# A fused attention and two-MoE kernel: which VectorE operation a GpSimd operation at the shared port waits for

## The chip, the cores and the metric

One core of a Trainium2 chip. The metric is the device time of one execution in microseconds; the time of a kernel is the median of its runs. Every row of a profile comes from one profiled execution. Engines are named as in the profile: PE (TensorE matmul), PEld (its weight load), DVE (VectorE), ACT (ScalarE), POOL (GpSimd), SP (SyncE, which issues the DMAs).

## The reference

Three parts follow one another. The attention has 4 batches of 8 heads, 576 positions, 64 channels; scores below the row's maximum less `tau` are cut off before the softmax:

```python
scores = scale * np.matmul(q, k.transpose(0, 1, 3, 2))
thresh = np.max(scores, axis=-1, keepdims=True) - tau
scores = np.where(scores >= thresh, scores, -1000000000.0)
attn = softmax(scores)          # exp of the difference to the maximum, divided by the sum
x = matmul(attn, v)             # then laid out as 2304 tokens x 512
x = g(x @ w_in) @ w_out         # g(h) = h * clip(h + 3, 0, 6) / 6;    512 -> 2048 -> 512
out = g2(x @ w2_in) @ w2_out    # g2(h) = h / (1 + exp(-1.702 h));     512 -> 2048 -> 512
```

## The kernel before

The data are float32. To use the faster float32r matmul, an operand is split into a high part (rounded, by ScalarE or VectorE) and a low part (the difference, a subtraction by GpSimd or VectorE), and a product is three matmuls: high by high, high by low, low by high. The weights arrive as 64-bit numbers and are decoded on the chip (`decode`, L559): two copies on ScalarE, three operations on VectorE (L586, L587, L588) and an addition on GpSimd (L589); then they are split (`split`, `split_to`, `combined`).

In time there are three stages. Up to about 410 us the heads are worked in 16 pairs (`unit`, L721): scores on TensorE, maximum and masked exponentials on VectorE and ScalarE (`soft`, L838), the sums' reciprocals and the scaling on GpSimd and VectorE (`norm`, L861), a transposition, the product with V, and the first half of the first MoE (`moe_a`, L1099) mixed in between. From 410 to 650 us the second half of the first MoE runs (`moe_b`, `wide`), while the second MoE's weights are decoded and combined. From 650 us on the second MoE runs in blocks of 512 tokens (one of 256), each with seven products of half-size matrices in place of eight (`moe2`, `hidden2`, `gate2`; their sums and differences `c`, `u`, `p` are made by VectorE and GpSimd).

No engine's order is left to a scheduler. Each operation is entered in a `Plan` (L178) with its engine, a cost, what it reads and writes, and sometimes an alternative engine; `SWAPS` picks the alternatives. `Plan.order` (L229) goes through time with these costs and the latencies `LAT` between engines (L25; from VectorE to GpSimd 155), picks the next operation of each engine by a stored rank (`RANKS`), and leaves a planned start for each. The program is written out in the order of these starts. The sets `PORT` (L35) name the operations that use the SBUF port which VectorE and GpSimd share: while one engine has such an operation, the planner does not start one on the other (L262), and lets it start at exactly the moment the other one ends:

```python
if port[o] and taken[DVE + POOL - e] > t:
    est[o] = taken[DVE + POOL - e]
```

`Plan.fill` (L369) is what carries this into the program. For each GpSimd operation at the port (L394) it looks up the last VectorE operation (of any kind) whose entry in `ends` is not after the GpSimd operation's planned start (plus 0.5), and `tie` (L1628) adds a semaphore wait for it. VectorE is not made to wait for GpSimd in this way. `ends` is what the change touches; `busy` (L1634), also called from `fill`, puts a few idle matmuls into the first 60 us.

Of the kernel before, what the change touches and what calls it, by code (L numbers as in the profile page):

```python
# [22 lines left out]
PE, ACT, DVE, POOL, SP, DMA = range(6)  # L23

LAT = {  # L25
    (PE, PE): 0, (PE, ACT): 197, (PE, DVE): 197, (ACT, PE): 200, (ACT, ACT): 200, (ACT, DVE): 150, (ACT, POOL): 170,
    (DVE, PE): 200, (DVE, ACT): 120, (DVE, DVE): 127, (DVE, POOL): 155, (POOL, PE): 203, (POOL, ACT): 200, (POOL, DVE): 220, (POOL, POOL): 130,
    (SP, DMA): 53, (ACT, DMA): 53, (DMA, PE): 943, (DMA, ACT): 943, (DMA, DVE): 943, (DMA, POOL): 1000, (DMA, SP): 943,
}
# [148 lines left out]
class Plan:  # L178
# [190 lines left out]
    def fill(self, order, make):  # L369

        made, dve = {}, [o for o in order if o.eng == DVE]
        ends = [self.start[o.n] + o.cost + LAT[DVE, POOL] for o in dve]

        def keep(op):
            return lambda: made.__setitem__(op.n, op.fn())

        def behind(op, i):
            return lambda: self.tie(op.fn(), next((made[o.n] for o in dve[i::-1] if made[o.n] is not None), None))

        used = [[] for _ in range(BANKS)]  # L380
        for b in self.banks:
            ops = [x[0] for x in b.access]
            used[b.bank].append((min(self.start[o.n] for o in ops), max(self.start[o.n] + o.cost for o in ops) + 250))
        out, end = [], 0.0
        for op in order:
            if op.eng == PE:
                t, s = end, self.start[op.n]
                end = max(end, s + op.cost)
                count = int((s - t) / 450 if s < 12000 else (s - t - 300) / 216)
                if count > 0:  # L390
                    slack = max((min([t - y for _, y in u if y <= t] + [1e9]), -i) for i, u in enumerate(used) if not any(x < s and y > t for x, y in u)) if any(not any(x < s and y > t for x, y in u) for u in used) else None
                    if slack is not None:
                        out.append(make(-slack[1], count))
            i = bisect_right(ends, self.start[op.n] + 0.5) - 1 if op.eng == POOL and self.port[op.n] else -1  # L394
            out.append(keep(op) if op.eng == DVE else behind(op, i) if i >= 0 else op.fn)
        return out
# [1301 lines left out]
```

## Time and profile before

| what | value |
| --- | --- |
| median of 3 runs (1028.32, 1028.89, 1031.9) | 1028.89 us |
| profiled execution, its own time | 1031.23 us |
| its span, first to last instruction | 1029.4 us |
| TensorE busy | 1016.6 us |
| VectorE busy | 792.3 us |
| ScalarE busy | 667.9 us |
| GpSimd busy | 566.3 us |

Busy time is time in which an engine has an instruction under way; a record of GpSimd or VectorE also holds the time in which it stands at the port. Matmuls are pipelined and each record is longer than the distance to the next, so a TensorE that is busy in the records can still lose a little between matmuls. In the list of waits a row names who waited, for whom, the sum in us, how often, and the longest. A wait for several semaphores is put down to the one that came last. In the timeline a row is: start, duration, engine, line, operation, out<-in, and in brackets the idle time of the engine before it with what ended it. Operations that a helper makes carry the helper's line (L534 is `tt`, L531 is `copy`), so they are told apart by their tiles.

### The profile page before, as it was taken

Reading aid. Unit: us, or ns where it says so; the run is one execution under the profiler, and the core shown is the slowest. Engines: PE = TensorE matmul, PEld = TensorE weight load, DVE = VectorE, ACT = ScalarE, POOL = GpSimd, SP = SyncE. Lnnn points to the kernel's source line nnn. Section 1 sums busy time; section 2 is a strip of 40 time slices with the busy share of each in tenths; the row PEclk is TensorE's granted clock in tenths of the full one; section 3 lists DMA queues with packets and bytes.
Section 4 is the critical chain, followed back from the end, with each engine's and each line's share of the span. In section 5 each row is a group of like instructions: output and inputs, shape, how many; then the busy total and the mean of one; then the engine's idle time right before and its main releaser. Section 6 shows DMA issues by size and latency. Waiting matters only on the chain.

```text
span 1029.4 us, 21355 instructions
## 1 busy us (share of the span) xinstructions
PE 1016.6 (99%) x7560; PEld 950.0 (92%) x7560; DVE 792.3 (77%) x1700; ACT 667.9 (65%) x1395; POOL 566.3 (55%) x681
## 2 busy tenths in 40 slices
PE   8999999999999999999999999999999999999998
PEld 7787888798979898999999999999999999999998
DVE  7999999997999994667876687656677997555544
ACT  5988678676777674766444344667757767555553
POOL 5577866675756562666564435445654535446452
PEclk9999999999999999999999999999999999999999
DMA  8344466686877665445746778937464896443412
GB/s 242 118 118 126 140 186 189 170 233 171 223 212 200 199 188 165 143 142 182 206 149 178 242 230 266 310 105 258 148 204 168 280 317 198 143 165 110 144 45 73
DMA packets 113195, 187.47 MB, mean 182 GB/s; under 512 B 10816, under 2 KB 62656, under 8 KB 111040
## 3 DMA queue, kind: packets, MB, share of 16 engines
q1 hardware_dynamic: 112944, 185.80, 58.7%
q8 instruction: 60, 0.98, 0.4%
q14 instruction: 47, 0.39, 0.1%
q10 hardware_dynamic: 144, 0.29, 0.1%
HBM read 117.77 MB, written 68.29 MB: 181 GB/s over the span
## 4 chain that ended last, share of the span: by engine, by line
PE 90%; DVE 4%; DMA 2%; ACT 1%; POOL 1%; issue 1%; SPq 0%; DVEq 0%; POOLq 0%; ACTq 0%
PE pm L1306 18%; PE py L1442 11%; PE pm L1072 11%; PE py L1097 10%; PE pm L1097 8%; PE pm L1187 7%; PE pm L1442 6%; PE ps L792 6%; PE pm L1010 5%; PE pm L918 3%; PE ps L816 1%; PE pm L994 1%; DVE e L852 1%; PE ps L832 1%; DVE nm L848 1%; DMA wrawstg<-in_w1o_dram 1%
## 5 line engine op out<-in xcount | busy, mean ns | idle before, releaser
L848 DVE TENSOR_REDUCE nm<-ps 128x1 f32<-128x576 f32 x144 | 106.2, 750 | 14.9 <-PE ps L792 10.2
L851 ACT ACTIVATE e<-ps,nm 128x576 f32<-128x576 f32 x128 | 93.2, 740 | 30.1 <-DVE nm L848 26.9
L534 POOL TENSOR_TENSOR g<-t,g 128x256 fp32r<-128x256 f32 (+2 forms) x84 | 74.4, 888 | 65.4 <-ACT g L531 19.1
L852 DVE SCALAR_TENSOR_TENSOR e<-ps,th,e 128x576 f32<-128x576 f32 x128 | 102.1, 811 | 6.9 <-ACT e L851 3.6
L1097 PE MATMUL pm<-g,outhring 128*128 128x256 f32 (+1 forms) x512 | 105.7, 299 | 0.0
L531 ACT ACTIVATE g<-t 128x256 fp32r<-128x256 f32 (+3 forms) x177 | 86.1, 489 | 20.9 <-DVE t L1084 10.5
L1072 PE MATMUL pm<-xh,inhring 128*128 128x256 f32 (+1 forms) x320 | 97.8, 306 | 0.3 <-DVE t L1084 0.2
L1097 PE MATMUL py<-g,outhring 128*128 128x432 f32 (+2 forms) x384 | 96.8, 336 | 0.0
L1072 PE MATMUL pm<-xh,inlring 128*128 128x256 f32 (+1 forms) x320 | 94.4, 295 | 0.0
L1072 PE MATMUL pm<-xl,inhring 128*128 128x256 f32 (+1 forms) x320 | 94.4, 295 | 0.0
L534 POOL TENSOR_TENSOR wmstg<-wmstg,wrstg 128x512 uint32<-128x512 uint32 x40 | 54.2, 1358 | 72.4 <-DVE wmstg L588 32.3
L792 PE MATMUL ps<-kqv 128*128 128x288 f32 x480 | 82.0, 302 | 2.2 <-DVE th L849 1.1
L1097 PEld LDWEIGHTS pm<-g,outhring 128*128 128x128 f32 x512 | 81.9, 189 | 0.8 <-issue 0.5
L792 PEld LDWEIGHTS ps<-kqv 128*128 128x128 f32 x480 | 68.2, 190 | 10.0 <-issue 4.5
L1097 PE MATMUL pm<-g,outlring 128*128 128x256 f32 (+1 forms) x256 | 75.6, 295 | 0.0
L1097 PEld LDWEIGHTS py<-g,outhring 128*128 128x128 f32 x384 | 68.7, 188 | 2.1
L1097 PE MATMUL py<-g,outlring 128*128 128x432 f32 (+2 forms) x192 | 64.6, 336 | 0.0
L1072 PEld LDWEIGHTS pm<-xh,inhring 128*128 128x128 f32 x320 | 60.6, 189 | 2.1 <-PE pm L1639 0.5
L1072 PEld LDWEIGHTS pm<-xl,inhring 128*128 128x128 f32 x320 | 60.6, 189 | 0.0
L534 POOL TENSOR_TENSOR kqv<-qk,kqv 64x576 fp32r<-64x576 f32 (+1 forms) x39 | 55.9, 1434 | 8.4 <-DVE g L534 2.5
L1072 PEld LDWEIGHTS pm<-xh,inlring 128*128 128x128 f32 x320 | 60.5, 189 | 0.0
L1358 ACT ACTIVATE pm<-id 128x256 f32<-128x256 f32 (+1 forms) x98 | 37.4, 387 | 30.8 <-DVE c L534 30.3
(265 smaller groups left out, 3615.9 us busy)
## 6 DMA issues: line engine op xcount, KB each, us to landing
turned<-tr SPq DMA_DIRECT2D x16, 1024.0 KB, 4.1
et<-turned SPq DMA_DIRECT2D x64, 256.0 KB, 5.7
wrawstg<-in_w1i_dram SPq DMA_DIRECT2D x16, 512.0 KB, 4.0
wrawstg<-in_w1o_dram SPq DMA_DIRECT2D x16, 512.0 KB, 3.6
wrawstg<-in_w2i_dram SPq DMA_DIRECT2D x16, 512.0 KB, 4.0
wrawstg<-in_w2o_dram SPq DMA_DIRECT2D x16, 512.0 KB, 4.2
qk<-in_k_dram SPq DMA_DIRECT2D x24, 288.0 KB, 3.9
qk<-in_q_dram SPq DMA_DIRECT2D x24, 288.0 KB, 4.3
```

The costliest lines, as they stand in the source:

```text
L531: return lambda: nc.scalar.activation(out=o(), in_=i(), func=ACTF.Copy, **kw)
L534: return lambda: (nc.vector if eng == DVE else nc.gpsimd).tensor_tensor(out=o(), in0=a(), in1=b(), op=op)
L792: nc.tensor.matmul(ps.t[:, i, :SH], q, w[hd].t[:, i * SH:(i + 1) * SH], start=a, stop=z)
L848: add(DVE, 672, K("R", s), "R", lambda: nc.vector.tensor_reduce(out=nm.t[:, c], in_=ps.t[:, :, :SH], op=ALU.max, axis=AX.XY, negate=True), ...
L851: add(ACT, 624, K("X", s), "X", lambda: nc.scalar.activation(out=ev(), in_=ps.t[:, :, :SH], func=ACTF.Exp, bias=nm.t[:, c]), [ps, (nm, s)] ...
L852: add(DVE, 736, K("M", s), "M", lambda: nc.vector.scalar_tensor_tensor(out=ev(), in0=ps.t[:, :, :SH], scalar=th.t[:, c], in1=ev(), op0=ALU ...
L1010: nc.tensor.matmul(pv[p].t[64 * hd:64 * hd + 64, :CH[p][1]], v_(k, hd), et_m(p, turned)[:, hd, k], start=k == 0, stop=False)
L1072: nc.tensor.matmul(ph.t[:, :n], a, v, start=(cc == 0 and i == 0), stop=(cc == KC - 1 and i == 2))
L1097: nc.tensor.matmul(py.t[:, :n], a, v, start=(st and i == 0), stop=(sp and i == 2))
L1187: nc.tensor.matmul(ph.t[:, :n], a, v, start=(cc == 0 and q == 0), stop=(cc == KC - 1 and q == 2))
L1306: nc.tensor.matmul(half(i)(), u.t[:, ws], v.t[:, xv], start=False, stop=True, skip_group_check=True)
L1442: nc.tensor.matmul(to, u.t[:, ws], v.t[:, at:at + n], start=(st and j == 0 and cc == 0 and o is not None), stop=(sp and j == 2), skip_grou ...
```

## The change

The latency from VectorE to GpSimd is no longer added to the planned end of a VectorE operation in `fill`. The lookup for a GpSimd operation can then find a later VectorE operation: one that is planned to end up to 155 before the GpSimd operation's planned start, or exactly at it. Ranks, costs, planned starts and the order of every engine stay as they are.

```diff
     def fill(self, order, make):
 
         made, dve = {}, [o for o in order if o.eng == DVE]
-        ends = [self.start[o.n] + o.cost + LAT[DVE, POOL] for o in dve]
+        ends = [self.start[o.n] + o.cost for o in dve]
 
         def keep(op):
             return lambda: made.__setitem__(op.n, op.fn())
```

## Rows read from the trace of the kernel before

**Rows 1.** The page's first part: busy us, share of the span, instructions.

```profile
PE 1016.6 (99%) x7560; PEld 950.0 (92%) x7560; DVE 792.3 (77%) x1700; ACT 667.9 (65%) x1395; POOL 566.3 (55%) x681
```

**Rows 2.** Busy us by stage: stretch, length, engines, PEclk, DMA share, GB/s.

```profile
0.00:60.00 60.00, 56.30 (x361) 44.12 (x362) 52.59 (x135) 45.06 (x83) 32.55 (x58) 1.00 0.57 171
60.00:250.00 190.00, 187.71 (x1432) 160.88 (x1431) 175.93 (x429) 147.40 (x301) 134.01 (x192) 1.00 0.61 173
250.00:410.00 160.00, 158.77 (x1215) 140.31 (x1214) 136.58 (x324) 105.84 (x219) 87.12 (x145) 1.00 0.68 190
410.00:650.00 240.00, 239.80 (x1453) 233.50 (x1452) 179.37 (x341) 128.73 (x239) 130.44 (x108) 1.00 0.63 194
650.00:1029.00 379.00, 374.06 (x3110) 371.22 (x3108) 247.88 (x473) 240.86 (x557) 182.17 (x179) 1.00 0.53 177
```

Engines in each row: PE, PEld, DVE, ACT, POOL.

**Rows 3.** The page's chain that ended last, by engine.

```profile
PE 90%; DVE 4%; DMA 2%; ACT 1%; POOL 1%; issue 1%; SPq 0%; DVEq 0%; POOLq 0%; ACTq 0%
```

**Rows 4.** Waits of TensorE from 0 to 410 us, two of ten.

```profile
PE ps L792 <- DVE th L849: 1.1, 1, 1.1
...
PE ps L816 <- DVE th L849: 0.8, 1, 0.8
```

**Rows 5.** Waits of TensorE from 410 us to the end, all of them.

```profile
PE pm L1306 <- ACT pm L1358: 0.7, 2, 0.3
PE pm L1072 <- DVE t L1084: 0.2, 1, 0.2
```

**Rows 6.** Timeline at 837 us: VectorE, GpSimd and ScalarE.

```profile
836.87 0.68 DVE L534 TENSOR_TENSOR outlring<-outlring,outhring 128x512 fp32r<-128x512 f32 x1
...
837.48 0.68 DVE L534 TENSOR_TENSOR gl<-c,g 128x512 fp32r<-128x512 f32 x1
...
837.70 1.06 POOL L534 TENSOR_TENSOR c<-t,c 128x256 f32<-128x256 f32 x1 [5.15 <-DVE outlring L534]
...
838.79 0.63 ACT L531 ACTIVATE g<-c 128x512 fp32r<-128x512 f32 x1 [0.37 <-POOL c L534]
```

**Rows 7.** GpSimd's operations on tile c: count, ns min/median/max, first and last.

```profile
L534 POOL TENSOR_TENSOR c<-t,c x28: 727/790/1192, 665.0 to 997.3; 128x256 f32<-128x256 f32 x28
```

**Rows 8.** Timeline at 433 us: VectorE, then GpSimd.

```profile
433.37 0.69 DVE L588 SCALAR_TENSOR_TENSOR wmstg<-wrawstg,wmstg 128x512 uint32<-128x512 uint32 x1
...
434.13 1.41 POOL L534 TENSOR_TENSOR wmstg<-wmstg,wrstg 128x512 uint32<-128x512 uint32 x1 [1.45 <-DVE wmstg L588]
```

**Rows 9.** Timeline at 514 us: VectorE, GpSimd and TensorE.

```profile
514.62 0.41 DVE L587 TENSOR_SCALAR wmstg<-wmstg 128x512 uint32<-128x512 uint32 x1
514.85 1.17 POOL L534 TENSOR_TENSOR g<-t,g 128x432 fp32r<-128x432 f32 x1 [0.83 <-DVE yc L534]
515.07 1.49 DVE L588 SCALAR_TENSOR_TENSOR wmstg<-wrawstg,wmstg 128x512 uint32<-128x512 uint32 x1
...
516.13 0.56 PE L1097 MATMUL py<-g,outhring 128*128 128x432 f32 x2
```

**Rows 10.** VectorE's L586 and L588: as lines (busy, mean), then as sources (min/median/max).

```profile
L588 DVE SCALAR_TENSOR_TENSOR wmstg<-wrawstg,wmstg 128x512 uint32<-128x512 uint32 x56 | 43.7, 783 | 0.4
...
L586 DVE TENSOR_SCALAR wmstg<-wmstg 128x512 f32<-128x512 f32 x56 | 31.1, 557 | 7.5 <-ACT wmstg L585 7.4
...
L588 DVE SCALAR_TENSOR_TENSOR wmstg<-wrawstg,wmstg x56: 673/686/1495, 15.6 to 634.2; 128x512 uint32<-128x512 uint32 x56
...
L586 DVE TENSOR_SCALAR wmstg<-wmstg x56: 413/424/1449, 14.6 to 632.8; 128x512 f32<-128x512 f32 x56
```

**Rows 11.** Waits of SyncE's queue on GpSimd, two of many.

```profile
SPq L760 <- POOL kqv L534: 29.7, 12, 6.0
...
SPq L575 <- POOL wmstg L534: 26.4, 10, 6.2
```

**Rows 12.** The chain from 64 to 82 us: start, us, what.

```profile
71.30 1.44 POOL wmstg L534
...
72.75 5.26 DMA wrawstg<-in_w1o_dram
```

## The prediction

> **What bounds the kernel now.** I read the page's busy line first, and under it the busy time by stage: TensorE is at work in 1016.6 of 1029.4 us, its granted clock 1.00 (2.4 GHz) throughout, and from 410 to 650 us it is busy 239.80 of 240 [rows 1, 2]. VectorE has 77% and GpSimd 55%, unevenly: from 60 to 250 us VectorE is busy 175.93 of 190 us (93%) and GpSimd 134.01. The chain of waits says the same in another way: 90% of the path that sets the end is TensorE, 4% VectorE, 1% GpSimd [rows 3]. What TensorE waits for outside its own queue is little: before 410 us it is idle 3.70, 2.29 and 1.23 us in the three stages, 7.2 us together, and its longest waits there are on VectorE's softmax (1.1 and 0.8 us); from 650 us on 4.9 us are idle, but only 0.9 us of waits are listed after 410 us, 0.2 of them on VectorE [rows 2, 4, 5]. So two things can move the end: a GpSimd result that TensorE is about to read comes later, which costs directly because TensorE has nothing to spare, or VectorE gets ahead in the first 410 us, which can give back part of 7.2 us and no more.
>
> **What the change does to one operation.** The plan in the code (start and cost of each operation as `order` leaves them) has 677 operations on GpSimd, 634 of them at the port. For 293 of these a VectorE operation is planned to end within the 155 that the diff takes out, so their wait moves to a later VectorE operation, in 284 cases the next one. In 204 of them the plan started GpSimd exactly at the end of a VectorE port operation: the change makes it wait for that one. No instruction or DMA is added, no queue changes order: only the counts waited for.
>
> What such a moved wait costs is seen at 837.70 us [rows 6]. The GpSimd `c<-t,c` had sat idle for 5.15 us for `outlring`, which it does not read: that is the old tie. `outlring` ended at 836.87 + 0.68 = 837.55, GpSimd began 0.15 us later, while VectorE's `gl<-c,g` ran until 837.48 + 0.68 = 838.16. GpSimd's record took 1.06 us where the same operation takes 0.73 at least [rows 7], and ended at 838.76, which is 0.60 us after `gl`. So it stood at the port, but its first 0.13 to 0.14 us (0.73 or 0.74 less 0.60) were already behind it. Waiting for `gl` instead, it starts a handover after 838.16 and runs its whole length. The handover was 0.15 us here and 0.07 us at 434.13 (after 433.37 + 0.69) [rows 6, 8]; so it ends at 838.96 to 839.05, 0.20 to 0.29 us later. I take 0.23, nearer the lower end, because the 0.07 followed an operation of the weight decoder, whose operations are the most moved kind (71 of the 293). Below, the bound is nothing, where VectorE has already ended; above it is the next term.
>
> The Trainium skill (SBUF — State Buffer, section "Who interferes with whom") says that the pair is locked for a whole instruction and the one that issues second "fully blocks". Taken to the letter GpSimd would do all of its 0.73 us after 838.16 and end at 838.89, not at the 838.76 of the trace; the wait would then add 0.07 to 0.15 us an operation, not 0.20 to 0.29. The trace disagrees by those 0.13 us.
>
> **Where the order at the port turns.** A second price is at 514.85 us [rows 9]. The GpSimd `g<-t,g` began while VectorE's L587 ran (514.62 to 515.03), so it was first in line: L588, issued at 515.07, took 1.49 us against a median of 686 ns [rows 10]. Waiting for L587, GpSimd starts at 515.10 at the earliest, behind L588. L588 then takes 0.69 us and ends at 515.76, and GpSimd, which ended 0.99 us after VectorE let go (516.02 less 515.03), ends at 516.75 instead of 516.02: 0.73 us later, while VectorE gains 0.80. The reader of that `g` is the pair of matmuls at 516.13, the second of which, at about 516.33, needs the low half. It would now start at some 516.83: TensorE stands 0.5 us. In the plan the VectorE operation behind the new tie is again a port operation in 49 of the 293 cases. How many of these turn I estimate from the time that L586 and L588 are held: means of 557 and 783 ns against medians of 424 and 686, 56 each, are 12.9 us [rows 10], at 0.7 us apiece some 18 operations. Most of their GpSimd partners are weights or products with time to spare; I take six to be read soon enough to count: two for about 0.5 us (the pattern of 514.85 returns at 615.83), four for 0.1 to 0.3, whose readers come 0.2 to 0.4 us later.
>
> **Who waits behind the waiting instruction.** GpSimd's own queue is in order, so a late operation makes its next one late unless it idles between; SyncE's queue waits for GpSimd to free the staging buffers of K, Q and the raw weights (29.7 and 26.4 us) [rows 11], and ScalarE takes `c` for its rounding (it sat idle 0.37 us for it at 838.79) [rows 6]. In the stretch from 410 us on GpSimd is busy about half the time, which lets 0.23 us drain before the next product is due.
>
> **The sum.** Plain lateness: if four in five of the 293 are held, some 230 operations by 0.23 us are about 53 us of waiting, on an engine that idles 463 us now (1029.4 less 566.3); on TensorE I put it at 0.3 us, for a handful of products that are read within a quarter of a microsecond (lower bound 0, upper some 15 such places, 3.5 us). Turned order: 2 x 0.5 + 4 x 0.2 = 1.8 us; each stall also gives the later products time, so I keep 1.5. VectorE wins time in the turned cases, about half of the 12.9 us, but most of that lies after 410 us, where TensorE waits for VectorE 0.2 us in all [rows 5]: worth nothing on the path. Sum: +1.8 us, from -1 (a little of the 7.2 us comes back, nothing lost) to +5.3. The profiled execution has 1031.23 us around a span of 1029.4; that makes 1033.0 for it. It lies 2.3 us over the median of the runs, 1028.89, so the median I forecast is 1030.7. A measurement of this kernel tells about 0.5%, 5.1 us, from no change; this is inside.
>
> **Rivals.** (a) *Slower by more than that: lateness carried by the queues into the loads of the first 410 us.* Four loads stand in the chain (at 72.75, 118.52, 243.13 and 405.86 us); the first is issued right after a GpSimd `wmstg` of 1.44 us at 71.30 and takes 5.26 us to land, with TensorE waiting behind it [rows 12]. GpSimd is 71% busy from 60 to 250 us, so lateness can pile up: five moved operations in a row are 1.15 us, at four loads 4.6, with the 1.8 above 6.4: 1035.3. It decides from four moved operations in a row ahead of each load. For it: the SyncE waits [rows 11]. Against it: GpSimd idles for microseconds between its bursts, and the operations on the chain at these loads are mostly not moved ones. (b) *Faster: VectorE, relieved, pulls the attention stages in.* If half of the 7.2 us and the DMA waits behind it came back it would be 1024 to 1025. Against it: the blocked VectorE time lies elsewhere, and lateness on GpSimd adds to the same chains (its reciprocal waits for GpSimd's sum). (c) *The change does nothing that matters*: GpSimd stood blocked at the port for as long as it now waits for the count, so that only a handover of 0.07 to 0.15 us is new, and the places that TensorE reads early have more spare than I read: 1028.9, or 0.2 more. For it: every moved operation with a port operation ahead was indeed held. Against it: the 0.60 us above. By the Trainium skill's rule cited above it would be this case as far as plain lateness goes.
>
> **The numbers.** My forecast has 0.58, (a) 0.16, (b) 0.06, (c) 0.20. The first and (c) are within 0.5%, (a) is nearly all slower, (b) nearly all faster: faster 0.05, same 0.79, slower 0.16. The range holds the first and (c) with their bounds, and a part of (a): 1027.5 to 1035.0.
>
> **What would show it.** In the profile after: GpSimd's busy time falls by some 30 to 50 us (held time leaves its records) with the maxima of `c<-t,c` and `wmstg` nearer their minima; L588 near 515 us has 0.69 instead of 1.49; the means of L586 and L588 fall toward the medians; the `g` near 515 us ends 0.7 us later against L587, and a gap of some 0.5 us stands in TensorE before the pair that reads it. TensorE's idle time after 410 us rises by 1 to 3 us. I am wrong in kind if TensorE's new idle time is before 410 us and behind DMAs (a), if its idle time there falls (b), or if GpSimd's operations end no later against VectorE's than now (c).

## The result, and the profile after

The median is 1037.43 us (1036.97 to 1038.43, 4 runs) against 1029.64 (1028.32 to 1031.9, 4 runs) of the kernel before: a ratio of 1.0078 with a 95% interval of 1.0062 to 1.0094, some 8.0 us slower. The interval is clear of no change, and the median lies outside the forecast's range. The two profiled executions, 1036.98 and 1031.23 us, are 5.75 apart, because that of before lies 1.6 above its median and that of after 0.4 below; what follows on traces has only these 5.75 us to find. No engine's order changed, only the counts waited for.

The page's busy line, to be read against [rows 1]:

```profile
PE 1020.4 (99%) x7560; PEld 950.0 (92%) x7560; DVE 809.0 (78%) x1700; ACT 669.1 (65%) x1395; POOL 545.4 (53%) x681
```

GpSimd's records lost 20.9 us, time in which it stood at the port. VectorE's gained 16.7, which the forecast had the other way round. TensorE is busy 3.8 us longer over the same 7560 matmuls, so most of the loss does not appear as idle time. The busy time by stage, columns as in [rows 2]:

```profile
0.00:60.00 60.00, 56.08 (x360) 43.91 (x361) 52.73 (x135) 44.88 (x83) 32.12 (x57) 1.00 0.58 171
60.00:250.00 190.00, 187.36 (x1425) 160.16 (x1425) 178.35 (x428) 146.88 (x300) 133.44 (x193) 1.00 0.59 173
250.00:410.00 160.00, 158.93 (x1209) 139.68 (x1208) 136.88 (x325) 105.72 (x219) 84.77 (x145) 1.00 0.67 189
410.00:650.00 240.00, 238.73 (x1442) 230.88 (x1441) 183.64 (x338) 127.92 (x236) 122.21 (x106) 1.00 0.61 192
650.00:1035.00 385.00, 379.26 (x3132) 375.41 (x3130) 257.41 (x478) 243.67 (x561) 172.82 (x181) 1.00 0.53 177
```

TensorE's idle time by stage is 3.92, 2.64, 1.07, 1.27 and 5.74 us, 14.6 in all against 12.4; the clock is the same. To see when the time is lost I take the last matmul of one kind in each stage: the last of the attention's `pm<-et,kqv`, the last L1187, and the last L1442 (count, ns min/median/max, first and last start). Before:

```profile
L1187 PE MATMUL pm<-xh,inhring x128: 352/359/362, 505.0 to 647.1; 128*128 128x432 f32 x128
L1014 PE MATMUL pm<-et,kqv x96: 376/428/480, 138.7 to 402.3; 64*64 64x256 f32 x48, 64*64 64x320 f32 x48
...
L1442 PE MATMUL py<-g,outlring x160: 276/279/287, 674.9 to 1024.6; 128*128 128x256 f32 x160
```

and after:

```profile
L1187 PE MATMUL pm<-xh,inhring x128: 352/358/362, 508.4 to 651.4; 128*128 128x432 f32 x128
L1014 PE MATMUL pm<-et,kqv x96: 376/428/481, 139.3 to 403.7; 64*64 64x256 f32 x48, 64*64 64x320 f32 x48
...
L1442 PE MATMUL py<-g,outlring x160: 276/279/287, 679.4 to 1030.3; 128*128 128x256 f32 x160
```

The lag is 1.4 us at the end of attention (403.7 less 402.3), 4.3 at the last L1187 and 5.7 at the end: 1.4, 2.9 and 1.4 us by stage. In the middle stage a reason can be seen. The list of what the weight loads of TensorE waited for from 410 to 650 us had no GpSimd in it before:

```profile
PEld pm L1072 <- DVE t L1084: 0.4, 1, 0.4
PEld pm L1072 <- ACT t L531: 0.2, 1, 0.2
```

It is now


```profile
PEld py L1097 <- POOL g L534: 2.2, 5, 0.6
PEld pm L1097 <- POOL g L534: 0.5, 1, 0.5
PEld py L1097 <- DVE yc L534: 0.4, 1, 0.4
```

The readers of `g` themselves, on the page (busy, mean ns, then idle time before them), before:

```profile
L1097 PE MATMUL pm<-g,outhring 128*128 128x256 f32 (+1 forms) x512 | 105.7, 299 | 0.0
...
L1097 PE MATMUL py<-g,outhring 128*128 128x432 f32 (+2 forms) x384 | 96.8, 336 | 0.0
```

and after:

```profile
L1097 PE MATMUL pm<-g,outhring 128*128 128x256 f32 (+1 forms) x512 | 106.3, 299 | 0.4 <-POOL g L534 0.3
...
L1097 PE MATMUL py<-g,outhring 128*128 128x432 f32 (+2 forms) x384 | 98.4, 339 | 1.0 <-POOL g L534 0.7
```

These two groups alone are busy 0.6 + 1.6 us longer and idle 0.4 + 1.0 us before their start: 3.6 of the 5.75 us. Some 60% of that is inside records, because a record of several matmuls runs on while the second waits for its weights.

In the attention stage the weight loads had no wait for GpSimd before, and now have

```profile
PEld pm L918 <- POOL er L867: 0.6, 2, 0.4
PEld pm L918 <- POOL e L867: 0.2, 1, 0.2
```

The longest of them shows how a late operation reaches TensorE through GpSimd's queue (GpSimd, then the weight load):

```profile
189.07 1.44 POOL L534 TENSOR_TENSOR kqv<-qk,kqv 64x576 fp32r<-64x576 f32 x1 [0.70 <-DVE rc L859]
...
193.76 0.53 PEld L918 LDWEIGHTS pm<-id,er 128*128 128x128 f32 x5 [0.41 <-POOL er L867]
```

Against VectorE's masked exponential behind it (start 190.18 us before, 190.75 now) `kqv` starts 0.29 us later than before (188.21 us before). From there GpSimd works on through `pk`, two `e`, `sm`, `pk` and `er`, with at most 0.1 us between two of them in both traces. In the plan only `kqv` of these has a moved wait. `er` starts at 192.96 us (192.11 before), 0.28 us later against VectorE, and the weight load that reads it waits 0.41 us.

Two spots of before return. At 842 us, the place of [rows 6] (VectorE, then GpSimd):

```profile
842.40 0.68 DVE L534 TENSOR_TENSOR gl<-c,g 128x512 fp32r<-128x512 f32 x1
843.00 0.68 DVE L534 TENSOR_TENSOR yc<-py,yc 128x512 f32<-128x512 f32 x1
843.60 0.90 DVE L534 TENSOR_TENSOR outlring<-outlring,outhring 128x512 fp32r<-128x512 f32 x1
...
843.22 0.74 POOL L534 TENSOR_TENSOR c<-t,c 128x256 f32<-128x256 f32 x1 [5.31 <-DVE gl L534]
```

`c` now waits for `gl`, starts 0.14 us after its end and takes 0.74, so it ends 0.88 us after `gl` where it was 0.60: 0.28 us later. But it now stands in front of VectorE's next port operation, `outlring`, which took 0.90 us instead of 0.68. At 517 us, the place of [rows 9] (VectorE, GpSimd, TensorE, weight loads):

```profile
517.26 0.99 DVE L587 TENSOR_SCALAR wmstg<-wmstg 128x512 uint32<-128x512 uint32 x1
518.28 0.69 DVE L588 SCALAR_TENSOR_TENSOR wmstg<-wrawstg,wmstg 128x512 uint32<-128x512 uint32 x1
518.89 1.61 DVE L534 TENSOR_TENSOR outlring<-wmstg,outhring 128x512 fp32r<-128x512 f32 x1
...
518.41 1.53 POOL L534 TENSOR_TENSOR g<-t,g 128x432 fp32r<-128x432 f32 x1 [0.46 <-DVE wmstg L587]
...
519.54 0.93 PE L1097 MATMUL py<-g,outhring 128*128 128x432 f32 x2
...
520.00 0.19 PEld L1097 LDWEIGHTS py<-g,outhring 128*128 128x128 f32 x1 [0.46 <-POOL g L534]
```

L588 has its 0.69 us, as forecast; `g` ends at 519.94, 1.69 us after L587 against 0.99 before; the weight load waits 0.46 us for it, and the pair of matmuls takes 0.93 us instead of 0.56. The 0.80 us that VectorE won at L588 is gone one operation later: `outlring` takes 1.61 us (0.68 before). L587 itself takes 0.99 us where it took 0.41, since a GpSimd `wmstg` that ends at 517.96 us now stands before it; before, that hold was on L586 (1.25 us, now 0.70). The same over the kernel, GpSimd's `c` (as in [rows 7]) and VectorE's L588 and L586 (as in [rows 10]):

```profile
L534 POOL TENSOR_TENSOR c<-t,c x28: 731/739/1095, 669.7 to 1003.2; 128x256 f32<-128x256 f32 x28
```

```profile
L588 DVE SCALAR_TENSOR_TENSOR wmstg<-wrawstg,wmstg 128x512 uint32<-128x512 uint32 x56 | 43.4, 777 | 0.4
...
L586 DVE TENSOR_SCALAR wmstg<-wmstg 128x512 f32<-128x512 f32 x56 | 32.3, 578 | 5.1 <-ACT wmstg L585 4.7 <-POOL wmstg L534 0.2
```

The median of `c` fell from 790 to 739 ns; VectorE's means, 783 and 557 before, did not both fall: 777 and 578.

### The profile page after: what moved, and what is told of

Read it like the earlier page. It is cut to its first block, busy times and chain, and to the rows that moved or that the text cites. A ratio compares the mean times of both kernels' runs of the same rounds, so it can differ in the third digit from the quotient of the medians.

```text
span 1035.1 us, 21354 instructions
## 1 busy us (share of the span) xinstructions
PE 1020.4 (99%) x7560; PEld 950.0 (92%) x7560; DVE 809.0 (78%) x1700; ACT 669.1 (65%) x1395; POOL 545.4 (53%) x681
## 4 chain that ended last, share of the span: by engine, by line
PE 73%; DVE 14%; issue 4%; ACT 4%; DMA 3%; POOL 2%; POOLq 0%; DVEq 0%; ACTq 0%; SPq 0%
PE pm L1306 15%; PE py L1442 9%; PE pm L1097 8%; PE py L1097 7%; PE pm L1072 7%; PE pm L1187 6%; PE pm L1442 6%; PE ps L792 5%; PE pm L1010 4%; PE pm L918 2%; DVE e L852 2%; DVE nm L848 2%; DVE wmstg L588 1%; POOL g L534 1%; DVE wmstg L586 1%
```

## Experiments

Where a run moves only a part of the 293 waits it has, in `fill`, beside the old `ends`, the diff's own sum under another name, and takes the later VectorE operation only where a condition holds:

```diff
+        soon = [self.start[o.n] + o.cost for o in dve]
-            i = bisect_right(ends, self.start[op.n] + 0.5) - 1 if op.eng == POOL and self.port[op.n] else -1
+            i = j = -1
+            if op.eng == POOL and self.port[op.n]:
+                i = bisect_right(ends, self.start[op.n] + 0.5) - 1
+                j = bisect_right(soon, self.start[op.n] + 0.5) - 1
+                if CONDITION:
+                    i = j
```

Each run below gives its condition as the added line. The ratio is to the kernel before on the same chip, with its 95% interval; 0.001 of it is 1.03 us. In the rows of these kernels that are shown here the line numbers are higher by 6.

### Which stage

```diff
+                if self.start[op.n] < 402e3:
```

> The later wait only for GpSimd operations planned in the attention stage (131 of the 293 moved waits), all others as before. Against the kernel before, of the whole change's +8.0 us: theory A (TensorE loses where it reads a GpSimd product that has become late, step by step, most of it between 410 and 650 us) expects +1 to +2.5 us here; theory C (lateness is carried by GpSimd's and SyncE's queues into the loads of the first 410 us) expects +5 us or more; theory B (VectorE is held longer at the port and that is what costs, most where it is held most, after 650 us) expects +0 to +1.5.

Measured: 1.0019 (1.0006 to 1.0031), +2.0 us.

```diff
+                if 402e3 <= self.start[op.n] < 640e3:
```

> The later wait only for GpSimd operations planned between 410 and 650 us (71 of the moved waits, all of them behind a VectorE port operation). Theory A: +3 to +4 us, with gaps of 0.3 to 0.6 us in TensorE near 423, 458, 489, 500, 517 and 618 us. Theory B: about +1.5. Theory C: less than +1.

Measured: 1.0032 (1.0021 to 1.0044), +3.3 us. The waits of its weight loads from 410 to 650 us:

```profile
PEld py L1103 <- POOL g L540: 2.6, 5, 0.9
PEld pm L1103 <- POOL g L540: 0.8, 2, 0.5
PEld py L1103 <- DVE yc L540: 0.4, 1, 0.4
```

```diff
+                if self.start[op.n] >= 640e3:
```

> The later wait only for GpSimd operations planned after 650 us (91 of the moved waits). Theory A: +1 to +2 us. Theory B: +4 us or more. Theory C: 0 to +0.5. If the three stages add up, the sum of the three differences is 8.0 us within about 1.5.

Measured: 1.0004 (0.9993 to 1.0016), +0.4 us. Its busy line, and its chain by engine:

```profile
PE 1015.1 (99%) x7560; PEld 949.0 (92%) x7560; DVE 800.7 (78%) x1700; ACT 667.1 (65%) x1395; POOL 553.1 (54%) x681
...
PE 77%; DVE 9%; DMA 6%; issue 3%; ACT 3%; POOL 1%; SPq 1%; POOLq 0%; DVEq 0%; ACTq 0%
```

What follows: the 71 waits of the middle stage, all behind port operations, cost most, and nearly the same GpSimd waits as after the whole change stand in front of the products. The 131 of the attention stage cost 2 us, the 91 of the last stage nothing that these runs can tell. VectorE is held 8.4 us longer in that last one (800.7 less 792.3) and has 9% of the chain instead of 4% [rows 3], and the time hardly moves: VectorE's held time and its share of the chain are not the price there. The three parts give 5.7 us, the whole 8.0; with intervals of some 1.2 us on each part and 1.6 on the whole that is no contradiction, but an interaction of up to a few us isn't excluded.

### No tie at all

```diff
-            i = bisect_right(ends, self.start[op.n] + 0.5) - 1 if op.eng == POOL and self.port[op.n] else -1
+            i = -1
```

> No GpSimd operation waits for VectorE for the port's sake; only the waits for data are left. If the wait itself is the cost and the port sorts things out, this is faster than before by 1 to 3 us. If the waits keep GpSimd from running ahead of VectorE operations that the plan puts first (theory: the old tie to the operation before is worth having), VectorE's busy time rises by 20 us or more over 792 and the time is longer than before by 3 us or more.

Measured: 1.0124 (1.0103 to 1.0146), +12.8 us.

```profile
PE 1021.4 (98%) x7560; PEld 951.0 (91%) x7560; DVE 828.8 (79%) x1700; ACT 665.7 (64%) x1395; POOL 577.1 (55%) x681
```

VectorE is held longest here, and GpSimd's records grow too: both engines stand at the port in an order that nobody chose. The ties as they were are worth 12.8 us. The 8.0 us of the change are not a part of these: without ties GpSimd's busy time rises by 10.8 us against the kernel before, while with the later ties it falls by 20.9.

### Which operations

```diff
+                if not self.port[dve[j].n]:
```

> The later wait only where the VectorE operation now waited for is not at the port (77 of the 293 moved waits, nearly all in the attention stage and after 650 us). GpSimd gains nothing at the port by such a wait. If plain lateness by a handover is a good part of the loss: +1 to +2 us against the kernel before. If the loss comes from the waits behind port operations (their added 0.2 to 0.3 us and the turned order at the port): 0 to +0.7 us.

Measured: 1.0011 (0.9999 to 1.0023), +1.1 us for 77 waits: not told from nothing.

```diff
+                if op.name == "GL":
```

> The later wait only for the low halves of the MoE products (GL, 57 of the 293 moved waits), which TensorE reads next. Theory A (TensorE loses where it reads a late product): +3.5 to +5.5 us, most of it between 410 and 650 us. If the loss goes by the number of moved waits, through the queue of GpSimd: 57/293 of 8.0, +1.6 us.

Measured: 1.0018 (1.0008 to 1.0028), +1.9 us for 57 waits, the products that TensorE reads. In this run's profile three waits of the whole change's weight loads return, there 0.48, 0.39 and 0.56 us long near 424, 491 and 621 us:

```profile
422.67 0.19 PEld L1103 LDWEIGHTS pm<-g,outhring 128*128 128x128 f32 x1 [0.47 <-POOL g L540]
...
489.31 0.19 PEld L1103 LDWEIGHTS py<-g,outhring 128*128 128x128 f32 x1 [0.39 <-POOL g L540]
...
620.15 0.19 PEld L1103 LDWEIGHTS py<-g,outhring 128*128 128x128 f32 x1 [0.56 <-POOL g L540]
```

Ahead of each of these products GpSimd stands idle in the profile of the whole change:

```profile
423.43 1.15 POOL L534 TENSOR_TENSOR g<-t,g 128x256 fp32r<-128x256 f32 x1 [0.45 <-DVE wmstg L587]
...
490.01 1.18 POOL L534 TENSOR_TENSOR g<-t,g 128x256 fp32r<-128x256 f32 x1 [1.30 <-DVE wmstg L587]
...
619.95 1.53 POOL L534 TENSOR_TENSOR g<-t,g 128x432 fp32r<-128x432 f32 x1 [3.42 <-DMA kept<-wmstg]
```

So here it is the product's own wait that TensorE feels, not what stands before it in GpSimd's queue. (In the third row the idle time is put down to a DMA; VectorE's L587, the new tie, ended 0.18 us before `g` began.)

```diff
+                if op.name != "GL":
```

> The later wait for all GpSimd port operations but the low halves of the MoE products (236 of the 293 moved waits). Theory A: +2 to +4 us, from the attention stage and from decoded weights that hold up GpSimd's queue ahead of a product. By the number of moved waits: +6.4 us. This and the one before add up to 8.0 us within 1.5 if the two do not work through each other.

Measured: 1.0044 (1.0029 to 1.0058), +4.5 us for the other 236. By their numbers alone 57 of 293 would have 1.6 of the 8.0 us, and 236 would have 6.4. So the products have about their share and no more, and the view that the whole loss is theirs falls. To see what others cost, the 49 weight operations of the middle stage alone:

```diff
+                if 402e3 <= self.start[op.n] < 640e3 and op.name != "GL":
```

> The later wait only for the 49 GpSimd operations between 410 and 650 us that decode and split weights, none for the products' low halves. TensorE reads none of their results within the stage's next microsecond, so a loss can come only through GpSimd's own queue, which hands the products on later. If the queue matters: +1 to +2.5 us, with waits of TensorE for GpSimd's g. If only the later wait of the product itself matters: under +0.5 us.

Measured: 1.0022 (1.001 to 1.0034), +2.3 us, and among the waits of its weight loads from 410 to 650 us

```profile
PEld py L1103 <- POOL g L540: 2.4, 2, 2.2
```

No product's own wait was moved here, and yet the time is longer: by the times of the runs these 49 make 2.3 (1.0 to 3.5) of the middle stage's 3.3 us. The waits listed do not say how. The 2.2 us are one wait, in the slowest execution of this kernel (1034.63 us, its median 1031.99), and the chain that leads to it starts with a load of raw weights (the wait, then a piece of the chain):

```profile
518.65 0.19 PEld L1103 LDWEIGHTS py<-g,outhring 128*128 128x128 f32 x1 [2.17 <-POOL g L540]
...
505.98 7.36 DMA wrawstg<-in_w2i_dram
```

The same load landed after 5.9 us in the profile before, which has no such wait. Profiles of runs that move no wait in this stage have it too: 1.7 us in the run of the attention stage alone, where the load took 7.1 us, and 0.9 in the run of the last stage alone, at 6.9. So this wait comes with a late load, and this profile does not show what the 49 add to it.

### Turned at the port, or only late

```diff
+                if j + 1 < len(dve) and self.port[dve[j + 1].n]:
```

> The later wait only where the VectorE operation right behind the one now waited for is a port operation too (49 of the 293 moved waits, 23 of them between 410 and 650 us): there VectorE can get to the port ahead of GpSimd, and GpSimd is late by that operation as well. If the turned order is the dear part of the change: +2.5 to +4 us. If every moved wait costs alike: 49/293 of 8.0, +1.3 us.

Measured: 1.0025 (1.0013 to 1.0038), +2.6 us for the 49 waits whose next VectorE operation is at the port, the forecast's turned order.

```profile
PE 1016.7 (99%) x7560; PEld 949.5 (92%) x7560; DVE 790.7 (77%) x1700; ACT 667.5 (65%) x1395; POOL 566.2 (55%) x681
```

```diff
+                if j + 1 < len(dve) and not self.port[dve[j + 1].n]:
```

> The later wait in the other 244 cases, where the operation behind is not at the port, so that GpSimd only starts later by the handover and its own first part. If the turned order is the dear part: +3 to +5 us. If every moved wait costs alike: +6.7 us. With the run before this one it adds up to 8.0 within 1.5 if the two parts do not work through each other.

Measured: 1.0052 (1.004 to 1.0064), +5.3 us for the other 244, the plain lateness of the forecast.

```profile
PE 1018.1 (99%) x7560; PEld 950.6 (92%) x7560; DVE 813.2 (79%) x1700; ACT 668.1 (65%) x1395; POOL 546.9 (53%) x681
```

Among the waits of this run's weight loads is the same place as in the run of the 49, with the load landing after 5.7 us (GpSimd, then the weight load):

```profile
517.89 1.30 POOL L540 TENSOR_TENSOR wmstg<-wmstg,wrstg 128x512 uint32<-128x512 uint32 x1 [1.25 <-DVE wmstg L592]
519.14 1.30 POOL L540 TENSOR_TENSOR g<-t,g 128x432 fp32r<-128x432 f32 x1
...
520.50 0.19 PEld L1103 LDWEIGHTS py<-g,outhring 128*128 128x128 f32 x1 [0.50 <-POOL g L540]
```

Before, GpSimd stood idle for 0.83 us ahead of this `g` [rows 9]. Here a weight operation (`wmstg`, a moved wait) runs right up to it, and `g`, whose own wait is not moved in this run, is late for TensorE by 0.50 us.

The two runs give 7.9 us, the whole change 8.0. All of VectorE's and GpSimd's shift of busy time is in the second (VectorE 792.3 to 813.2, GpSimd 566.3 to 546.9), and so are two thirds of the loss. A further theory was that GpSimd, late, stands in front of VectorE's next port operation, as `c` did at 843 us, and that VectorE's readers pay. It was split by whether such an operation is planned within 300 behind GpSimd's planned end:

```diff
+        def follows(o, j):
+            k = next((k for k in range(j + 1, len(dve)) if self.port[dve[k].n]), None)
+            return k is not None and self.start[dve[k].n] - self.start[o.n] - o.cost < 300
+                if j + 1 < len(dve) and not self.port[dve[j + 1].n] and follows(op, j):
```

> Of the 244 moved waits without a turned order, only the 86 where VectorE's next port operation is planned to start as the GpSimd operation ends (within 300 of it), so that a late GpSimd holds VectorE at the port. If the +5.3 us of the 244 go through VectorE: +3.5 to +5 us, and VectorE's busy time goes up by 15 us or more over 792. If late products reach TensorE by themselves, alike for all: 86/244 of 5.3, +1.9 us.

Measured: 1.002 (1.0011 to 1.0029), +2.1 us for 86 waits; VectorE busy 806.0 us.

```diff
+                if j + 1 < len(dve) and not self.port[dve[j + 1].n] and not follows(op, j):
```

> The other 158 of the 244: no VectorE port operation is planned behind the GpSimd operation. If the loss goes through VectorE: 0 to +1.5 us, VectorE's busy time within 4 us of 792. If late products reach TensorE by themselves: +3.4 us.

Measured: 1.0024 (1.0013 to 1.0034), +2.5 us for 158; VectorE busy 801.0. By numbers the 5.3 us would split as 1.9 and 3.4. The intervals hold that, and they don't hold a loss that lies in the first part alone. VectorE's hold grows by 13.7 us in the first and 8.7 in the second, and the time doesn't follow it.

### Other allowances

```diff
-        ends = [self.start[o.n] + o.cost + LAT[DVE, POOL] for o in dve]
+        ends = [self.start[o.n] + o.cost + 2 * LAT[DVE, POOL] for o in dve]
```

> The allowance doubled (310 in place of 155), so that some GpSimd operations wait for a VectorE operation one earlier than in the kernel before. If the old wait is already early enough that GpSimd mostly reaches the port behind the right operation, an earlier wait lets it run ahead: between the kernel before and the one without waits (+13.9 us), I expect +2 to +5 us, and VectorE's busy time above 792 us by 5 or more. If lateness of GpSimd is still a loss in the kernel before, -1 to -2 us.

Measured: 0.9991 (0.9978 to 1.0004): not told from the kernel before, where a loss was expected.

```diff
+        ends = [self.start[o.n] + o.cost + 3 * LAT[DVE, POOL] for o in dve]
```

> The allowance tripled (465 in place of 155; 312 waits moved to an earlier VectorE operation, 158 with 310). With 310 the time was 0.9 us under the kernel before, not told from it. If what is left to win is the lateness of GpSimd behind the wait, this is -1 to -2.5 us. If GpSimd now runs ahead of port operations that the plan puts first: +1 to +4 us, and VectorE's busy time is over 797 us.

Measured: 1.0051 (1.0037 to 1.0066), +5.3 us. So 0 and 465 both lose, and from 155 to 310 it is level. Since the twofold allowance might have won in one stage what it lost in another, it was also tried after 640 of the plan alone and before 402 alone (there the later operation is looked up in a list `early`, the sum with `2 * LAT[DVE, POOL]`, in place of `soon`):

```diff
+                if self.start[op.n] >= 640e3:
```

> The allowance doubled (310) for GpSimd operations planned after 650 us, all others as before. If the 0.9 us of the doubled allowance are real and come from the stage where its trace gained most against that of before (after 516 us): -1 to -2 us. If they were chance: -0.5 to +0.5.

Measured: 0.9997 (0.9984 to 1.0009).

```diff
+                if self.start[op.n] < 402e3:
```

> The allowance doubled (310) for GpSimd operations planned before 410 us, all others as before. By the same reading 0 to -1 us; the attention stage lost 2.0 us by the later wait, so if lateness is still a loss there in the kernel before, -1 to -2.

Measured: 1.0 (0.9987 to 1.0012). Neither wins, and no version here beats the kernel before.

## Why the prediction was wrong

**What one moved wait costs was right at the places that were read.** 0.20 to 0.29 us was the estimate, 0.23 the value taken; at 843 us it is 0.28, near the upper end, and GpSimd's `c` gets its full length after the handover. The turned spot came out as written too: L588 at 0.69 us, `g` later by 0.70 (0.73 was forecast), a wait of 0.46 us for the weights of the second matmul of the pair that reads it. The "Turned order" term, 1.5 us, measured 2.6 (1.3 to 3.9) in the run that moves only those 49.

**The step that failed is the term "Plain lateness" in "The sum".** It put 53 us of waiting beside 463 us of GpSimd's idle time and charged TensorE 0.3 us "for a handful of products", those read within a quarter of a microsecond, with 3.5 as the upper bound. Measured alone it is 5.3 us (4.1 to 6.6), above that bound, and it makes most of the difference between +1.8 and +8.0. What was counted was direct readers. The runs show that most of the loss is not theirs: the 57 products alone cost 1.9 us (0.8 to 2.9), the other 236 operations 4.5 (3.0 to 6.0), of which 49 weight operations of the middle stage 2.3. One way on which these reach TensorE is seen at two places: `kqv` at 189 us of the changed kernel and `wmstg` at 518 us of the run of the 244 are late, what follows in GpSimd's queue has no idle time before it, and a weight load of TensorE waits 0.41 and 0.50 us for a result whose own wait was not moved. "In the stretch from 410 us on GpSimd is busy about half the time, which lets 0.23 us drain" averages over a stage; a product right behind a weight operation has no such half. But all the waits of weight loads for GpSimd in the profile of the 244 come to some 1.6 us. How the rest of the 5.3 us reaches TensorE stays open.

**The attention stage was forecast at nothing and costs 2.0 us.** Rival (a) had the place, but not the price or the form: it wanted 4.6 us through four loads. TensorE's idle time before 410 us grew from 7.2 to 7.6 us. The weight loads there wait 0.8 us for GpSimd's scaled exponentials, where they waited for none before; the rest of the 2.0 us was not traced to a place.

**"VectorE wins time in the turned cases" was wrong over the kernel.** L588 at 517 us won its 0.80 us and the next operation lost 0.93; VectorE's busy time rose by 16.7 us in all, and in the run of the turned waits alone it fell by 1.6, where half of 12.9 was forecast. A GpSimd operation that starts later also ends later, and the next VectorE operation at the port is held instead. That this alone slows the kernel was a theory which fell: VectorE held 8.4 us longer in the last stage cost 0.4 us, and the followed and the unfollowed waits differ by no more than what their numbers give.

**The signs named beforehand.** GpSimd's busy time was to fall by 30 to 50 us and fell by 20.9; TensorE's idle time after 410 us was to rise by 1 to 3 and rose by 1.9 (from 5.1 to 7.0). This last looked as forecast while the loss was three times as large, since the idle time leaves out what is lost inside the records of matmuls. The lag of the same matmul in both traces gave the whole loss.

## What to carry to other kernels

A wait of a quarter of a microsecond that is added hundreds of times on an engine should not be set against that engine's idle time over a stage. For each product read early, look at its own wait, and at what was moved in the burst that runs right up to it. A long wait in one profile is a cause of the change only if profiles of kernels without that part of the change don't have it, too. Idle time and shares of the chain of waits were poor prices for the loss here; compare the start of the same late matmul in the two traces. When a planned order is tied to measured latencies, test the allowance on both sides, as here with 0, 155, 310 and 465, before taking it out.

## What was unexpected in the hardware

A GpSimd operation that stands at the port while VectorE finishes is already part of the way: it ended 0.60 us after VectorE's operation [rows 6], while one of the same shape that waited for the count ended 0.88 after it, 0.14 of it the handover. At this place, tying to the earlier VectorE operation hid handover and start behind VectorE's work. That fits what the allowance was worth here; it was not measured by itself. The time held at the port does not vanish when one side is made to wait: GpSimd's records lost 20.9 us and VectorE's gained 16.7, and with no ties at all VectorE's gained 36.5 (828.8 less 792.3).
